# Splitting a group's query products in two and reordering the stretch up to the first output product

## Chip, cores and metric

The kernel runs on one core of one Trainium2 chip. The metric is the device time of one execution in microseconds (us). A core has five engines, each with its own queue of instructions that it works through in order: TensorE (PE in the profile, its weight loads PEld), VectorE (DVE), ScalarE (ACT), GpSimd (POOL) and SyncE (SP), which here issues nearly all transfers. Engines wait for each other through semaphores.

## What is computed

```
a  = S1 x,  b = S2 x            for each row x (32 values) of q and k;  S1, S2: 8 x 32
phi(x) = outer(a, b)            64 features
kv  = sum over s of phi(k_s) v_s     64 x 32,  for each batch (4) and head (4)
z   = sum over s of phi(k_s)
out_s = phi(q_s) kv / (phi(q_s) . z + 1e-6)
X = out as (4352, 128)          4 batches x 1088 rows, 4 heads x 32
H = X @ w_in                    128 x 2048
G = where(H > 0, H, exp(min(H, 0)) - 1)
Y = G @ w_out                   2048 x 128
```

The inputs come as 64-bit floats, so each number of a weight has a low and a high 32-bit word, from which the kernel makes a 32-bit float by bit operations.

## The kernel before

**Tiling.** The 4352 rows are worked in groups of 512 (eight half tiles of 64 rows), the last group shorter. `w_in` and `w_out` are cut into eight chunk pairs `cp` of 2 x 128 columns. For each group and chunk pair `mm1` forms two banks of H (`h`, 128 x 512, one per half `c`), `elu_a` runs two steps on ACT (the negative part, then the exponential), `elu_d` one on DVE (which frees the bank), and `mm2` or `mm2_seven` adds the product with `w_out`. From group 1 on the products with `w_out` go by seven block products in place of eight, whose sums POOL forms.

**Order.** Nothing is scheduled by a program: the kernel is one hand-written list of calls, and each engine gets its instructions in the order of that list. Buffers come from pools: PSUM tag `h` has four banks, `aux` two; an instruction that takes a bank waits until its last reader is done.

**Start.** Keys of batch 0 are turned, multiplied by S1 and S2 and put into kv (`KA_first`, L439, on PE). Then x of group 0 (`xg`) is needed, by two ways that meet:
- the products: `q2_out(0, i)` forms the 64 features of the queries, `q4_early(0, hh)` (L640) turns them on PE, `q4_out(0, hh)` copies them out (on ACT for hh 0, on DVE for hh 1). `KS_copy` (ACT), `KS_turn` (PE, L501) and `KS_out` (ACT, L504) turn kv. `q5_early` (L666) multiplies the two into `xps`.
- the denominators: `q2_prod`, `q2_sum`, `q2_rec` on DVE, `den_wide` (ACT, L648) spreads them, `den_turn` (PE, L656) turns them, `den_out` (ACT, L660) copies them into `dent`.

`q5_early_out(0, w)` (DVE, L678) multiplies `xps` by `dent` for half `w` of the group, and `mm1_first(c, ws)` and `mm1` follow.

**Group 1** has another way: `q1_second` (L549) forms, in eight products, both sketches and the z products of its queries in one bank `abwp`; `q1_second_out` (ACT, L556) copies it; `q2_prod(1)`, `q2_sum(1)`, `q2_rec(1)`, `q2_an(1)` and `q2_out(1, i)` on DVE make the features with the denominators already in them; `q4_early(1, hh)`, `q4_out(1, hh)`, `q5_early(1)` and `q5_early_out(1, w)` make its x. The query rows come to PE's layout by `transp(qT, "q", 0, t0, t1)` on DVE: the first call gives tiles 8 to 12, the second 13 to 16; products i = 0, 1 of `q1_second` read tiles 8 to 11, i = 2, 3 tiles 12 to 15.

**Weights.** `load_rest` has queued their loads on SP. `R1(step, n)` does one rounding step for entry n of `order`: entries 0 and 1 are `w_in` of chunk pairs 0 and 1, 2 and 3 their `w_out`, 4 and 5 `w_in` and `w_out` of pair 2, and 6 to 10 all of pairs 3 to 7. The steps are `strip` (L127 on DVE, L129 on ACT), `low` (ACT L142, or POOL L140), `floor` (DVE L132), `shift` (DVE L135), `round_s` (DVE L119), and `whole` (POOL L145), which gives the finished weight. `whole_half(0, c)` is `whole` for one half of entry 0. SP's next load of a pair (pair 7) waits until the buffer of pair 2 is free, that is for `whole` of entry 5.

Of the kernel before, what the change touches and what calls it, by code (L numbers as in the profile page):

```python
# [12 lines left out]
F32 = mybir.dt.float32  # L13
# [16 lines left out]
def kernel(  # L30
# [21 lines left out]
    nc = tc.nc  # L52
    B, H, S, D = q.shape
    R = S1.shape[0]
    P = 128
# [4 lines left out]
    NT = S // 64  # L60
# [148 lines left out]
    def whole_half(i, c):  # L209
        if wide:  # L210
            cp, w_in, w_out = order[i]
            o = (0 if w_in else 2 * P) + P * c
            whole(raw_w[cp][:, o:o + P], W[:, cp, o:o + P])
# [70 lines left out]
    def transp(dst, x, b, t0, t1):  # L284
        nc.vector.transpose(dst[b][:, t0:t1, :].rearrange("p t (a c) -> p c t a", c=2), hd[x, b][:, :, t0:t1, :])
# [148 lines left out]
    def KA_first(tiles, first, last):  # L434
        if first:
            kv_ps[0] = psum.tile([P, 512], F32, name="kv", tag="o1", bufs=1)
        for i in tiles:
            for h in range(H):
                nc.tensor.matmul(kv_ps[0][32 * h:32 * h + 32, :R * R], vt[0][:, (h * KT + i) * D:(h * KT + i + 1) * D],  # L439
                                 feats[0, i // 5][:, i % 5, h].rearrange("p i j -> p (i j)"),  # L440
                                 start=(first and i == tiles[0]), stop=(last and i == tiles[-1]),
                                 skip_group_check=True, tile_position=(0, 32 * h))
        if last:
            del feats[0, 0], feats[0, 1]
# [51 lines left out]
    def KS_copy():  # L496
        kd = feats["kd"] = work.tile([P, 2, R * R], F32, name="kd", tag="kd", bufs=1)
        nc.scalar.copy(kd[:], _ap(kv_ps[0][:, :R * R], [[0, 2], [1, R * R]]))

    def KS_turn():  # L500
        nc.tensor.transpose(kv_ps[0][:, 128:256], feats.pop("kd")[:].rearrange("p w f -> p (w f)"), ident[:])  # L501

    def KS_out():
        nc.scalar.copy(kvS[:].rearrange("p h d -> p (h d)"), kv_ps[0][:, 128:256])  # L504
# [36 lines left out]
                                 qT[b][:, t, :], SW[:, :, 2, :], skip_group_check=True, tile_position=(0, 64 * u))  # L541
        return p[:, :128].rearrange("p (t h r) -> p h t r", t=4, h=H)

    def q1_second():
        p = psum.tile([P, 512], F32, name="abwp", tag="h", bufs=4)
        for i in range(4):
            for u in range(2):
                b, t = half_tile(1, 2 * i + u)
                nc.tensor.matmul(p[64 * u:64 * u + 64, i * 96:i * 96 + 96], qT[b][:, t, :],  # L549
                                 SW[:].rearrange("p h x r -> p (h x r)"), skip_group_check=True,  # L550
                                 tile_position=(0, 64 * u))
        return p

    def q1_second_out(p):
        abw[1] = work.tile([P, H * 4, 3 * R], F32, name="abw1", tag="abq1", bufs=1)
        nc.scalar.copy(abw[1][:].rearrange("p (h t) y -> p h t y", h=H),  # L556
                       p[:, :384].rearrange("p (t h y) -> p h t y", t=4, h=H))
# [34 lines left out]
    def q2_prod(g, zq=None):  # L592
        m = H * (un[g] if g > 1 else qn[g])
        x = abw[g][:, :m, :]
        pw = pws[g % 2]
        if zq is None:
            nc.vector.tensor_mul(pw[:, :m, :R], x[:, :, R:2 * R], x[:, :, 2 * R:3 * R])
        else:
            nc.vector.tensor_mul(pw[:, :m, :R].rearrange("p (h t) r -> p h t r", h=H),
                                 x[:, :, R:2 * R].rearrange("p (h t) r -> p h t r", h=H), zq)  # L600

    def q2_sum(g):
        m = H * (un[g] if g > 1 else qn[g])
        den = feats["den", g] = work.tile([P, 8 * H], F32, name="den", tag="den")
        nc.vector.tensor_reduce(den[:, :m], pws[g % 2][:, :m], axis=AX, op=ADD)
# [26 lines left out]
    def q4_early(g, hh):  # L632
        if g not in qpT:
            qpT[g] = work.tile([P, H, 2, P], F32, name="qpT", tag="qpT", bufs=2)
        p = qtp[g, hh] = psum.tile([P, 512], F32, name="qtp", tag="aux")
        for h2 in range(2):
            for m in range(2):
                o = (h2 * 2 + m) * P
                r = (2 * hh + h2) * 4 + 2 * m
                nc.tensor.transpose(p[:, o:o + P], qp[g][:, r:r + 2].rearrange("p t i j -> p (t i j)"), ident[:])  # L640

    def q4_out(g, hh):
        (nc.vector.tensor_copy if g == 0 and hh else nc.scalar.copy)(
            qpT[g][:, 2 * hh:2 * hh + 2], qtp.pop((g, hh))[:].rearrange("p (h m s) -> p h m s", h=2, m=2))

    def den_wide():
        d = feats["denw"] = work.tile([P, 4, H, D], F32, name="denw", tag="ob", bufs=2)
        nc.scalar.copy(d[:], _ap(feats.pop(("den", 0))[:, :1], [[1, 4], [4, H], [0, D]]))  # L648

    def den_turn():  # L650
        p = feats["denp"] = psum.tile([P, 512], F32, name="denp", tag="h", bufs=4)
        d = feats.pop("denw")
        for w in range(2):
            for m in range(2):
                o = (2 * w + m) * P
                nc.tensor.transpose(p[:, o:o + P], d[:, 2 * m + w].rearrange("p h d -> p (h d)"), ident[:])  # L656

    def den_out():
        d = feats["dent"] = work.tile([P, 2, 2 * P], F32, name="dent", tag="cc", bufs=1)
        nc.scalar.copy(d[:].rearrange("p w s -> p (w s)"), feats.pop("denp")[:])  # L660

    def q5_early(g):
        xp = xps[g] = [psum.tile([P, 512], F32, name="xps", tag="aux") for _ in range(2)]
        for h in range(H):
            for w in range(2):
                nc.tensor.matmul(xp[w][D * h:D * h + D, :256], kvS[64 * w:64 * w + 64, h, :],  # L666
                                 qpT[g][64 * w:64 * w + 64, h].rearrange("p m s -> p (m s)"),
                                 skip_group_check=True, tile_position=(64 * w, D * h))

    def q5_early_out(g, w):  # L670
        if g not in xg:
            xg[g] = work.tile([P, 512], F32, name="xg", tag="xg", bufs=3)
        to = xg[g][:].rearrange("p (m w s) -> p w m s", w=2, s=P)
        x = xps[g][w][:, :256].rearrange("p (m s) -> p m s", s=P)
        if g:
            nc.scalar.copy(to[:, w], x)
        else:
            nc.vector.tensor_mul(to[:, w], x, feats["dent"][:, w].rearrange("p (m s) -> p m s", s=P))  # L678
# [238 lines left out]
    def mm1_first(c, ws):  # L917
        h = h_tile(0, 0, c)
        for w in ws:
            cols = [x[:].rearrange("p (m w s) -> p w m s", w=2, s=P)[:, w] for x in (h, xg[0])]  # L920
            quarters(cols[0], W[:, 0, c * P:c * P + P], cols[1])
# [138 lines left out]
    transp(qT, "q", 0, 8, 13)  # L1060
    q4_early(0, 0)
    KA_first(range(5, 9), False, True)
    q4_early(0, 1)
    q2_prod(0, zq)
    R1(strip, 0, nc.scalar)
    R1(low, 0)
    R1(strip, 1, nc.scalar)
    q4_out(0, 0)
    transp(qT, "q", 0, 13, NT)
    abwp = q1_second()  # L1070
    q2_sum(0)
    R1(floor, 0)
    KS_copy()
    KS_turn()
    q2_rec(0)
    den_wide()
    den_turn()
    q1_second_out(abwp)
    KS_out()
    R1(floor, 1)  # L1080
    R1(shift, 0)
    R1(shift, 1)
    q4_out(0, 1)
    R1(strip, 2, nc.scalar)
    den_out()
    R1(round_s, 1)
    q5_early(0)
    q2_prod(1)
    R1(low, 1, nc.gpsimd)
    R1(round_s, 0)  # L1090
    whole_half(0, 0)
    q2_sum(1)
    q5_early_out(0, 0)
    R1(low, 2)
    R1(low, 3)
    R1(low, 4)
    R1(strip, 3, nc.scalar)
    q5_early_out(0, 1)
    mm1_first(0, (0,))
    mm1_first(0, (1,))  # L1100
    elu_a(0, 0, 0, (0,))
    R1(strip, 4)
    q2_rec(1)
    R1(floor, 4)
    q2_an(1)
    R1(shift, 4)
    whole_half(0, 1)
    R1(whole, 1)
    mm1_first(1, (0, 1))
    elu_a(0, 0, 0, (1,))  # L1110
    q2_out(1, 1)
    mm1(0, 1, (1,))
    mm1(0, 1, (0,))
    q4_early(1, 1)
    R1(round_s, 4)
    q2_out(1, 0)
    elu_d(0, 0, 0)
    elu_a(0, 0, 1, (0,))
    q4_early(1, 0)
    elu_a(0, 0, 1, (1,))  # L1120
    elu_a(0, 1, 1, (0,))
    elu_a(0, 1, 1, (1,))
    elu_d(0, 0, 1)
    R1(whole, 4)
    mm1(0, 2, (0,))
    mm1(0, 2, (1,))
    R1(floor, 2)
    R1(shift, 2)
    R1(round_s, 2)
    q4_out(1, 1)  # L1130
    q4_out(1, 0)
    R1(strip, 7)
    elu_d(0, 1, 1)
    KT_out(0)
    elu_a(0, 1, 0, (0,))
    R1(floor, 3)
    R1(strip, 5)
    R1(whole, 2)
    elu_a(0, 2, 1, (0,))
    elu_a(0, 1, 0, (1,))  # L1140
    q5_early(1)
    q5_early_out(1, 1)
    q5_early_out(1, 0)
    mm2(0, 0, False, (0,))
    R1(shift, 3)
    R1(floor, 5)
    R1(low, 5)
# [826 lines left out]
```

## Time and profile before

| | us |
|---|---|
| median of 3 runs | 259.83 (259.80 to 260.07) |
| the profiled execution | 260.47 |
| its span | 258.33 |
| PE busy | 251.8 (97% of the span) |
| DVE, ACT, POOL busy | 174.6, 182.0, 184.1 |
| granted clock of PE | 0.997 |

The span is the time from the first to the last instruction of the profiled execution; 2.14 us lie around it. Times of the timeline count from the span's start. In a row of the timeline the first number is the start, the second the time from the first start to the last end of the rows merged (with the count after the x), and what stands in brackets is how long the engine sat idle before it and what it waited for. A 32-bit product on PE appears as two records, a turn by PE as one. Ends of PE's records are modelled.

### The profile page before, as it was taken

The page shows a single profiled execution, that of the slowest core. Times are in us where ns is not written, and L with a number is a line of the kernel's source. Part 1 is how long each engine was busy: PE and PEld are TensorE (multiplying, and loading weights), DVE is VectorE, ACT ScalarE, POOL GpSimd, SP SyncE. Part 2 cuts the span into 40 slices and gives each one's busy share as a digit, 9 for nine tenths or more (in the row PEclk, how much of TensorE's full clock was granted, in tenths as well). Part 3 has the DMA queues.
Part 4 walks back from the last instruction along what each step waited for, and adds up shares of the span by engine and source line. Part 5 has one row for each costly group of instructions (what it writes and reads, how often), then busy time and mean ns, then how long its engine had stood idle before and what let it go on. Part 6 is the DMA issues. An engine that isn't in the chain of part 4 may idle for free.

```text
span 258.3 us, 9778 instructions
## 1 busy us (share of the span) xinstructions
PE 251.8 (97%) x4101; PEld 159.8 (62%) x4101; DVE 174.6 (68%) x342; ACT 182.0 (70%) x357; POOL 184.1 (71%) x236
## 2 busy tenths in 40 slices
PE   8789999999999999999999999999999999999994
PEld 7653333426666677657648466666766666667994
DVE  5898998898859875797658587743455445644651
ACT  2589887748757657676577877578677777777792
POOL 5433365698994978877858887987888888888310
PEclk9999999999999999999999999999999999999998
DMA  6999593313000011114102004312021100110021
GB/s 178 303 366 238 177 285 65 95 23 55 7 5 4 15 18 27 25 35 105 35 13 31 0 7 94 83 39 33 11 32 28 19 3 0 24 20 3 3 33 31
DMA packets 30907, 16.56 MB, mean 64 GB/s; under 512 B 22512, under 2 KB 28016, under 8 KB 30864
## 3 DMA queue, kind: packets, MB, share of 16 engines
q1 hardware_dynamic: 29904, 15.04, 24.4%
q10 hardware_dynamic: 896, 0.84, 1.3%
q8 instruction: 32, 0.52, 0.9%
q14 instruction: 11, 0.09, 0.1%
q0 software_dynamic: 64, 0.07, 0.1%
HBM read 11.21 MB, written 2.36 MB: 53 GB/s over the span
## 4 chain that ended last, share of the span: by engine, by line
PE 94%; DMA 3%; ACTq 1%; ACT 0%; issue 0%; DVE 0%; DVEq 0%
PE h L259 46%; PE pb L839 18%; PE pa L839 15%; PE o L259 5%; PE ol L259 3%; DMA v<-in_v_dram 3%; PE kv L453 1%; PE qtp L640 1%; PE h L738 1%; PE h L574 1%; PE pb L815 1%; PE xps L666 1%; PE kv L439 1%; PE kfps L366 1%; ACTq L81 0%; PE h L726 0%
## 5 line engine op out<-in xcount | busy, mean ns | idle before, releaser
L938 DVE SCALAR_TENSOR_TENSOR gg<-e,h 128x512 f32<-128x512 f32 x128 | 85.8, 682 | 60.9 <-ACT e L932 49.6
L259 PE MATMUL h<-xg,W 128*32 128x512 f32 (+2 forms) x768 | 121.7, 584 | 0.7 <-DVE xg L678 0.7
L930 ACT ACTIVATE e<-h 128x512 f32<-128x512 f32 x128 | 74.7, 591 | 51.3 <-PE h L259 49.7
L795 POOL TENSOR_TENSOR tt<-gg 128x512 f32<-128x512 f32 x55 | 71.5, 1301 | 25.9 <-DVE gg L938 23.2
L932 ACT ACTIVATE e<-e 128x512 f32<-128x512 f32 x128 | 79.3, 630 | 3.2
L259 PEld LDWEIGHTS h<-xg,W 128*32 128x32 f32 (+1 forms) x768 | 34.8, 119 | 44.5 <-issue 32.9
L800 POOL TENSOR_TENSOR tt<-tt,gg 128x256 f32<-128x256 f32 x55 | 41.8, 762 | 3.1
L802 POOL TENSOR_TENSOR tt<-gg,tt 128x256 f32<-128x256 f32 x55 | 40.5, 738 | 3.4
L839 PEld LDWEIGHTS pa<-gg,W 128*64 128x64 f32 (+1 forms) x528 | 25.7, 125 | 25.9 <-issue 25.6
L839 PE MATMUL pa<-gg,W 128*64 128x128 f32 (+1 forms) x528 | 32.4, 273 | 0.0
L839 PE MATMUL pb<-tt,SS 128*64 128x128 f32 (+1 forms) x472 | 29.5, 273 | 0.0
L145 POOL TENSOR_TENSOR W<-W,raw 128x256 uint32<-128x256 uint32 (+2 forms) x12 | 11.6, 977 | 20.3 <-ACT e L932 4.5
L839 PE MATMUL pa<-tt,SS 128*32 128x128 f32 (+1 forms) x404 | 25.3, 273 | 0.0
L839 PEld LDWEIGHTS pb<-tt,SS 128*64 128x64 f32 (+1 forms) x472 | 22.7, 127 | 0.0
L839 PE MATMUL pb<-tt,W 128*64 128x128 f32 (+1 forms) x292 | 21.9, 273 | 0.0
L839 PE MATMUL pb<-gg,SS 128*64 128x128 f32 (+1 forms) x292 | 21.8, 273 | 0.0
L839 PEld LDWEIGHTS pa<-tt,SS 128*32 128x32 f32 (+1 forms) x404 | 17.0, 120 | 0.0
L259 PE MATMUL o<-gg,W 128*32 128x512 f32 x128 | 15.3, 593 | 0.0
L839 PEld LDWEIGHTS pb<-gg,SS 128*64 128x64 f32 (+1 forms) x292 | 13.9, 124 | 0.0
L839 PEld LDWEIGHTS pb<-tt,W 128*64 128x64 f32 (+1 forms) x292 | 13.9, 124 | 0.0
L991 DVE SCALAR_TENSOR_TENSOR gg<-e,h 128x256 f32<-128x256 f32 x16 | 6.6, 418 | 6.4 <-PE h L259 3.2
L259 PEld LDWEIGHTS o<-gg,W 128*32 128x32 f32 x128 | 4.1, 110 | 9.3 <-issue 7.1
(181 smaller groups left out, 268.9 us busy)
## 6 DMA issues: line engine op xcount, KB each, us to landing
raw<-in_moe_w_in_dram SPq DMA_DIRECT2D x8, 256.0 KB, 6.6
raw<-in_moe_w_out_dram SPq DMA_DIRECT2D x8, 256.0 KB, 6.4
raw<-qpF SPq DMA_DIRECT2D x30, 64.0 KB, 2.0
out_dram<-ob SPq DMA_DIRECT2D x112, 16.0 KB, 1.5
hd_k<-in_k_dram SPq DMA_DIRECT2D x3, 544.0 KB, 8.7
hd_q<-in_q_dram SPq DMA_DIRECT2D x3, 544.0 KB, 8.3
v<-in_v_dram SPq DMA_DIRECT2D x4, 288.0 KB, 8.8
v<-in_v_dram SPq DMA_DIRECT2D x3, 256.0 KB, 8.8
```

Source lines behind the costliest of these rows:

```text
L145: nc.gpsimd.tensor_tensor(dst.bitcast(U32), dst.bitcast(U32), words(raw)[0], op=ADD)
L259: nc.tensor.matmul(dst[c:c + tile], lhs[:, c:c + tile], rhs, skip_group_check=True, tile_position=(0, c), **kw)
L366: nc.tensor.matmul(ps[g2][32 * c:32 * c + 32, :32 * KT], Sxp[r].rearrange("p x c r -> p (x c r)"), kT[b][r, u * KT:u * KT + KT, 32 * w:32 ...
L439: nc.tensor.matmul(kv_ps[0][32 * h:32 * h + 32, :R * R], vt[0][:, (h * KT + i) * D:(h * KT + i + 1) * D], feats[0, i // 5][:, i % 5, h].re ...
L795: nc.gpsimd.tensor_tensor(_ap(ts[g, cp][:, 0], [[4 * P, 2], [P, 2], [1, P]]), _ap(gs[g, cp][:, 0, P:], [[4 * P, 2]] + us), _ap(gs[g, cp][: ...
L800: nc.gpsimd.tensor_tensor(t[:, 1], t[:, 2], quarter(g, cp, 0, 0), op=ADD)
L802: nc.gpsimd.tensor_tensor(t[:, 3], quarter(g, cp, 1, 0), t[:, 1], op=SUB)
L839: nc.tensor.matmul(bank[r:r + width[0], P * col:P * col + P], lhs[:, w:w + width[0]], rhs[:, u], start=(first and i in ((0,) if g == 1 els ...
L930: nc.scalar.activation(e, hs[g, cp][c][:, :n], RELU, scale=-1.0)
L932: nc.scalar.activation(e, e, EXP, scale=-1.0)
L938: nc.vector.scalar_tensor_tensor(gs[g, cp][:, c, :n], es[g, cp][:, c, :n], -1.0, hs[g, cp][c][:, :n], op0=ADD, op1=MAX)
L991: nc.vector.scalar_tensor_tensor(gs["last", k // 2][:, k % 2, :2 * P], es["last", k // 2][:, k % 2, :2 * P], -1.0, hs["last", k][:, :2 * P ...
```

## The change

`q1_second` takes a bank and a pair of product numbers, so that it can be called twice: products 0 and 1 directly behind the turns of group 0's features (`q4_early(0, 1)`) and ahead of `KS_turn`, products 2 and 3 behind `q5_early(0)` and ahead of `mm1_first`. No instruction is added or left out on any engine. The list of calls from `q4_early(0, 1)` to the first `mm2` is put in another order; everything behind it stays. For each engine the new order is:

- PE: `q4_early(0,1)`, `q1_second` (0, 1), `KS_turn`, `den_turn`, `q5_early(0)`, `q1_second` (2, 3), `mm1_first` three times, `mm1(0,1)` half 0 then 1, `q4_early(1,0)`, `q4_early(1,1)`, `mm1(0,2)` half 1 then 0, `q5_early(1)`, `mm2(0,0)`.
- ACT: `low` 0, `strip` 0, `strip` 1, `KS_copy`, `den_wide`, `q4_out(0,0)`, `KS_out`, `strip` 2, `den_out`, `strip` 3, `low` 3, `q1_second_out`, `low` 4, `low` 2, then the steps of elu.
- DVE: `floor` 0, `q2_prod(0)`, `shift` 0, `q2_sum(0)`, `q2_rec(0)`, `round_s` 0, `floor` 1, `q4_out(0,1)`, `shift` 1, the transpose of tiles 13 to 16, `round_s` 1, `floor` 2, `q5_early_out(0,0)` and `(0,1)`, `strip` 4, `q2_prod(1)`, `floor` 4, `q2_sum(1)`, `q2_rec(1)`, `q2_an(1)`, `shift` 4, `q2_out(1,0)`, `round_s` 4, `q2_out(1,1)`, `elu_d` of chunk pair 0, and so on.
- POOL: `whole_half(0,0)`, `whole_half(0,1)`, `low` 1, `whole` 1, `whole` 4, `whole` 2 (before: `low` 1 first).

The function, and the list down to the first steps of elu:

```diff
-    def q1_second():
-        p = psum.tile([P, 512], F32, name="abwp", tag="h", bufs=4)
-        for i in range(4):
+    def q1_second(p=None, half=(0, 1)):
+        p = p or psum.tile([P, 512], F32, name="abwp", tag="h", bufs=4)
+        for i in half:
...
+    R1(low, 0)
     q4_early(0, 1)
+    R1(strip, 0, nc.scalar)
+    abwp = q1_second(None, (0, 1))
+    R1(floor, 0)
     q2_prod(0, zq)
-    R1(strip, 0, nc.scalar)
-    R1(low, 0)
+    R1(shift, 0)
     R1(strip, 1, nc.scalar)
-    q4_out(0, 0)
-    transp(qT, "q", 0, 13, NT)
-    abwp = q1_second()
     q2_sum(0)
-    R1(floor, 0)
-    KS_copy()
-    KS_turn()
     q2_rec(0)
-    den_wide()
-    den_turn()
-    q1_second_out(abwp)
-    KS_out()
-    R1(floor, 1)
-    R1(shift, 0)
-    R1(shift, 1)
-    q4_out(0, 1)
-    R1(strip, 2, nc.scalar)
-    den_out()
-    R1(round_s, 1)
-    q5_early(0)
-    q2_prod(1)
-    R1(low, 1, nc.gpsimd)
     R1(round_s, 0)
     whole_half(0, 0)
+    whole_half(0, 1)
+    R1(floor, 1)
+    KS_copy()
+    den_wide()
+    KS_turn()
+    den_turn()
+    q4_out(0, 1)
+    q4_out(0, 0)
+    KS_out()
+    q5_early(0)
+    R1(strip, 2, nc.scalar)
+    R1(shift, 1)
+    transp(qT, "q", 0, 13, NT)
+    abwp = q1_second(abwp, (2, 3))
+    den_out()
+    R1(strip, 3, nc.scalar)
+    R1(round_s, 1)
+    R1(floor, 2)
+    q5_early_out(0, 0)
+    q5_early_out(0, 1)
+    R1(low, 1, nc.gpsimd)
+    R1(whole, 1)
+    mm1_first(0, (0,))
+    R1(low, 3)
+    mm1_first(0, (1,))
+    q1_second_out(abwp)
+    R1(low, 4)
+    R1(low, 2)
+    R1(strip, 4)
+    q2_prod(1)
+    mm1_first(1, (0, 1))
+    mm1(0, 1, (0,))
+    mm1(0, 1, (1,))
...
```

More of the change, by code (lines that the diff above doesn't have):

```diff
@@ L1081 @@
-    R1(shift, 0)
-    R1(shift, 1)
-    q4_out(0, 1)
-    R1(strip, 2, nc.scalar)
-    den_out()
-    R1(round_s, 1)
-    q5_early(0)
-    q2_prod(1)
-    R1(low, 1, nc.gpsimd)
     R1(round_s, 0)
     whole_half(0, 0)
-    q2_sum(1)
[L1093 to L1102, printed above, removed]
+    whole_half(0, 1)
+    R1(floor, 1)
+    KS_copy()
@@ L1103 @@
+    R1(low, 2)
[4 more added lines that the diff above has]
+    mm1(0, 1, (1,))
+    elu_a(0, 0, 0, (0,))
+    elu_a(0, 0, 1, (0,))
+    elu_a(0, 0, 0, (1,))
+    elu_a(0, 0, 1, (1,))
+    R1(floor, 4)
+    q2_sum(1)
     q2_rec(1)
-    R1(floor, 4)
     q2_an(1)
     R1(shift, 4)
[L1107 to L1110, printed above, removed]
+    elu_a(0, 1, 1, (0,))
+    q2_out(1, 0)
+    q4_early(1, 0)
+    elu_a(0, 1, 1, (1,))
@@ L1111 @@
+    R1(round_s, 4)
     q2_out(1, 1)
-    mm1(0, 1, (1,))
-    mm1(0, 1, (0,))
     q4_early(1, 1)
[L1115 to L1129, printed above, removed]
     q4_out(1, 1)
     q4_out(1, 0)
+    R1(whole, 4)
+    elu_a(0, 1, 0, (0,))
+    elu_d(0, 0, 0)
@@ L1132 @@
+    elu_d(0, 0, 1)
+    R1(shift, 2)
+    R1(strip, 5)
+    R1(round_s, 2)
+    mm1(0, 2, (1,))
+    mm1(0, 2, (0,))
+    R1(whole, 2)
+    q5_early(1)
+    mm2(0, 0, False, (0,))
     R1(strip, 7)
     elu_d(0, 1, 1)
+    elu_a(0, 2, 1, (0,))
     KT_out(0)
-    elu_a(0, 1, 0, (0,))
+    q5_early_out(1, 1)
+    elu_a(0, 1, 0, (1,))
     R1(floor, 3)
[L1137 to L1142, printed above, removed]
     q5_early_out(1, 0)
-    mm2(0, 0, False, (0,))
```

## The prediction

> **What bounds the kernel now.** I read the page first, then the chain of waits, then the waits of TensorE, then the timeline from 9 to 31 us.
>
> ```profile
> PE 251.8 (97%) x4101; PEld 159.8 (62%) x4101; DVE 174.6 (68%) x342; ACT 182.0 (70%) x357; POOL 184.1 (71%) x236
> PE 94%; DMA 3%; ACTq 1%; ACT 0%; issue 0%; DVE 0%; DVEq 0%
> ```
>
> TensorE (PE) is busy for 97% of the span and is 94% of the chain. Its own waits are these four:
>
> ```profile
> PE idle L267 <- PEq L1959: 0.8, 1, 0.8
> PE h L259 <- DVE xg L678: 0.7, 1, 0.7
> PE abqp L527 <- DVE qT L285: 0.7, 1, 0.7
> PE kv L439 <- DMA v<-in_v_dram: 0.7, 1, 0.7
> ```
>
> Three lie before 10 us, where the change does nothing. The fourth, the wait for group 0's x (xg), is the last: behind it the stream stays closed to the end. So what the change is worth is how much earlier the first product with x starts, less whatever new hole it opens. The timeline shows what ends that wait:
>
> ```profile
> 12.80 0.88 PE L549 MATMUL abwp<-SW,qT 128*64 128x96 f32 x16
> 13.62 0.33 PE L501 MATMUL kv<-ident,kd 128*128 128x128 f32 x1
> 13.73 0.48 ACT L556 COPY abw<-abwp 128x384 f32<-128x384 f32 x1 [0.54 <-PE abwp L549]
> 13.78 0.60 PE L656 MATMUL denp<-ident,denw 128*128 128x128 f32 x4
> 14.11 0.27 ACT L504 COPY kvS<-kv 128x128 f32<-128x128 f32 x1
> 14.27 0.45 ACT L129 ACTIVATE W<-raw 128x256 f32<-128x256 f32 x1
> 14.43 0.67 PE L666 MATMUL xps<-qpT,kvS 64*32 64x256 f32 x16
> 14.61 0.58 ACT L660 COPY dent<-denp 128x512 f32<-128x512 f32 x1
> 15.26 0.76 DVE L678 TENSOR_TENSOR xg<-xps,dent 128x256 f32<-128x256 f32 x2 [0.17 <-PE xps L666]
> 15.83 3.96 PE L259 MATMUL h<-xg,W 128*32 128x256 f32 x48 [0.73 <-DVE xg L678]
> ```
>
> Sixteen records of group 1's eight query products (L549) stand ahead of the two turns (L501, L656). Their copy (L556) and a strip (L129) stand on ACT ahead of KS_out (L504) and den_out (L660). The first half of x waits for den_out (ends 15.19; x starts 15.26), which is later than the xps product (ends 15.10).
>
> **The change part by part.** Starts follow each other on ACT and DVE by about the duration less 0.1 (the 0.57 copy at 11.95, the next at 12.41); a result reaches ACT or DVE after 0.06, PE after 0.15 (x ends 15.68, PE starts 15.83); a dependent DVE op starts 0.08 behind.
>
> *PE ahead of x.* The first half keeps 8 of 16 records: four pairs at 0.08, so 0.33 less, and the turn of KS starts at 13.29 instead of 13.62, ending 13.62. Its input kd is there: the copy is freed of q4_out(0,0) and starts at KV's end, 12.28 + 0.06 = 12.34, over at 12.61. den_turn's place is 13.45. Its input hangs on q2_prod(0), now behind floor(0) on DVE, and floor(0) waits for strip(0), which goes behind low(0) on ACT (10.08 and 10.51, over at 10.96: in time). So floor 11.36, product 11.55, shift 11.72, sum 11.92, reciprocal 12.27, over at 12.51 (before 12.50, since a transpose left the chain). den_wide is thus where it was, 12.57 to 13.20; 0.15 makes 13.35, in time. den_turn ends 14.05.
>
> *ACT.* q4_out(0,0) 13.10 to 13.67. KS_out 13.67 to 13.94 (before 14.11). The xps products start at 13.99 (PE is free at 13.98), 0.44 earlier, and end at 14.66. strip(2) 13.83, den_out 14.17 to 14.76.
>
> *DVE up to x.* round_s(0) 12.43, floor(1) 12.77, copy q4_out(0,1) 12.95 (its transposes end 12.88), shift(1) 13.55, transpose 13..16, round_s(1), floor(2), then x: 0.28, 0.43, 0.42 and 0.25 less 0.08 each put x's place at 14.62. One wait is added, because POOL now works there: whole_half(0,0) and (0,1) run from 12.99 to 13.87 (0.46 each), then low(1). This row shows what a POOL op does to a DVE op of one tensor and a constant: strip(4), 0.28 elsewhere, took 0.81, ending 0.15 behind POOL's last op (16.59):
>
> ```profile
> 15.93 0.81 DVE L127 TENSOR_SCALAR W<-raw 128x256 uint32<-128x256 uint32 x1
> ```
>
> So shift(1) ends at 13.87 + 0.15 = 14.02 and x's place becomes 14.80. x starts at the latest of 14.80, 14.82 (dent) and 14.72 (xps): 14.82 instead of 15.26. PE's first product starts at 15.39 instead of 15.83: **0.44 gained**. That shift(1) slips in between two POOL ops is the choice here; the bounds are 14.72 (0.54 gained) and 15.22 (it also waits for low(1), 0.04 gained).
>
> The Trainium skill (SBUF — State Buffer, "Who interferes with whom") calls this an exclusive lock of a shared port pair, and holds DVE ops with two SBUF inputs to it as well, against a POOL op that reads SBUF. By that rule round_s(1), due at 14.30, waits for low(1), which itself began behind shift(1) (14.02 to 14.43); x's place becomes 14.90 and the gain 0.36. No row here shows such a DVE op held.
>
> *The second half.* PE has its place behind xps: 13.99 + 0.60 (the L666 at 22.59 to the next at 23.19) = 14.59; the transpose it needs is over at 14.35. Its last pair starts at 14.89, and with the 0.18 of a change of shape (13.43 to 13.62 ahead of L501) PE is free at 15.07. x comes at 15.39, so the half and its switch cost nothing; if x came at once, they would cost 0.48. The Trainium skill (TensorEngine Tiling, "Key Properties") says a change of tiling mode drains TensorE, which speaks against splitting: two more changes. By the rule the second half costs one more drain, by the rows it lies in the wait.
>
> *Behind x, group 1.* q1_second_out moves from 13.73 to 15.40 on ACT (behind strip(3) 14.64 and low(3) 14.98, whose loads landed by 13.0; over 15.88). Behind it wait low(4), low(2), then elu at 16.63, whose h is ready at 16.82: free. On DVE strip(4) is due at 15.5 and held behind whole(1) to 15.8, which costs nothing, since q2_prod(1) waits for that copy: it goes from 14.25 to 15.91, and the chain closes up: floor 16.12, sum 16.30, reciprocal 16.68, an 17.00, shift(4) 17.20, q2_out 17.41, round_s(4) 18.01, q2_out 18.35 to 19.03 (before 19.01). PE wants them at 19.28 and 19.72, so 0.5 is spare.
>
> *The rest to w_out.* First elu_d 18.95 to 19.63, second to 20.23; their banks (the four of tag h are taken here to come round in the order in which they come free) are wanted at 20.30 and 21.16. whole(4) ends 19.60, wanted 20.30; q4_out(1,·) ends 21.61, wanted 22.15; whole(2) about 22.0, wanted 22.75; xg of group 1 24.01, wanted 24.49. KT_out is queued earlier, but its transfers stand on SP behind the weight loads, which hold until 27.41 either way. mm1's halves change order at one price, the same records either way. strip(5) and strip(7) move ahead on DVE, into time that the elu before them leaves (20.35 and 20.90), their loads long landed. After the first w_out the order is the old one and PE closed, so 0.44 reaches the end.
>
> *Sum.* The profiled execution took 260.47: span 258.33 and 2.14 around it. The new span is 257.89, its execution 260.03. The median lies 0.64 under the profiled one, so **259.39**, 0.17% less.
>
> **Rivals.** *B, the columns start level.* From 15.83, 32 records of 256 columns and 16 of 512 should take 3.44 (24 of 512 take 2.57 from 24.93) plus 0.13 for the change to transposes (20.74 to 22.59 less 1.72): 3.57. They took 3.89 (15.83 to 19.72). One record starts at 15.83, the other column groups at 16.14. No producer is shown for this 0.32. For its loss: PE now comes fresh from other products. Against: xg's second half still follows 0.34 behind the first. Then 0.44 + 0.32 = 0.76, **259.07**.
>
> *C, shift(1) waits through low(1).* x starts 15.22, gain 0.04, **259.79**. For: three POOL ops stand back to back. Against: nothing shows that POOL keeps its turn.
>
> *D, slower: DVE's group 1 chain becomes the bound.* Strip(4), floor(4) and shift(4) now stand in the one chain ahead of q2_out, and q4_early(1,·) blocks mm1(0,2) on PE. If each of the three waits behind a POOL op of 0.74 to 1.07 (whole(1), whole(4)), q2_out ends up to 2 us later, 21.0 instead of 19.03. It decides from 0.54 later (19.57), and the kernel is slower from 0.98 later; at 1.5 later, a loss of 0.52, **260.35**. For: strip(4) was held before, and its cover (the spread of this chain from 14.25 on) is gone. Against: POOL has only whole(1) and whole(4) between 14.9 and 19.6.
>
> That the change does nothing is C's time.
>
> **How the numbers follow.** A 0.45, B 0.25, C 0.10, D 0.20. Under 0.2% (0.52 us) no measurement of this kernel tells a change from none. A spans 0.3 to 0.6, one third of it over 0.52: 0.15 faster, 0.30 same. B is faster (0.25). C is 0.08 same and 0.02 slower. D is slower (0.20). So 0.40, 0.38 and 0.22. The range runs from 259.0 (B, with 0.07 for the spread of runs) to 260.2, which takes in C and the lower part of D and leaves out about 0.15. A's own range is 259.2 to 259.55.
>
> **What would show it.** Right: KS_out at 13.7, xps at 14.0, den_out at 14.2, x at 14.8, the first h at 15.4, no hole in PE behind it, and L549 in two stretches at 12.8 and 14.6. Wrong: x behind 15.0 with a long L135 on DVE beside POOL's L140 (C); transposes L640 of group 1 or mm1(0,2) behind a wait for DVE near 19.7 (D); columns level at the first h (B). A hole in PE after 23 us would make all of it wrong.

## The result, and the profile after

| | before | after |
|---|---|---|
| median of 22 runs each | 259.82 us | 259.18 us |
| ratio of the times, 95% interval | | 0.9971 [0.9961, 0.9980] |
| the profiled execution | 260.47 us | 259.66 us |
| its span | 258.33 us | 257.76 us |

The kernel is faster by 0.29%: by 0.75 us, between 0.52 and 1.01, if the ratio is laid on 259.82. (One run of after, 262.79 us at a granted clock of 0.987 where the others show 0.997 to 1.0, was disturbed and is not in the ratio.)

First the page of after, its line of busy time and the one of the chain. They hardly moved, and PE still carries the chain:

```profile
PE 252.1 (98%) x4101; PEld 159.6 (62%) x4101; DVE 174.6 (68%) x342; ACT 182.1 (71%) x357; POOL 183.8 (71%) x236
...
PE 93%; DMA 4%; DVE 1%; issue 0%; ACTq 0%; SPq 0%; ACT 0%
```

Next PE's waits in after. The third row is the one that counts: the wait for x, 0.7 before, is 0.3, and no new wait for DVE or ACT stands beside it. The others lie ahead of 10 us.

```profile
PE abqp L527 <- DVE qT L285: 0.9, 1, 0.9
PE idle L267 <- PEq L1960: 0.8, 1, 0.8
PE h L259 <- DVE xg L678: 0.3, 1, 0.3
PE kv L439 <- issue: 0.2, 1, 0.2
```

Last the timeline of after, the rows that answer to those of before, with the turns of group 0's features (L640 at 12.18, 12.22 before) as the mark to count from, and POOL's two rows:

```profile
12.18 0.66 PE L640 MATMUL qtp<-ident,qp 128*128 128x128 f32 x4
...
12.77 0.55 PE L549 MATMUL abwp<-SW,qT 128*64 128x96 f32 x8
...
12.91 0.88 POOL L145 TENSOR_TENSOR W<-W,raw 128x128 uint32<-128x128 uint32 x2 [2.09 <-DVE W L119]
...
13.25 0.33 PE L501 MATMUL kv<-ident,kd 128*128 128x128 f32 x1
13.42 0.60 PE L656 MATMUL denp<-ident,denw 128*128 128x128 f32 x4
13.49 0.45 DVE L135 TENSOR_SCALAR W<-W 128x256 uint32<-128x256 uint32 x1
13.62 0.27 ACT L504 COPY kvS<-kv 128x128 f32<-128x128 f32 x1
13.76 0.48 POOL L140 TENSOR_SCALAR raw<-raw 128x256 f32<-128x256 uint32 x1
...
13.95 0.66 PE L666 MATMUL xps<-qpT,kvS 64*32 64x256 f32 x16
14.13 0.57 ACT L660 COPY dent<-denp 128x512 f32<-128x512 f32 x1
...
14.54 0.55 PE L549 MATMUL abwp<-SW,qT 128*64 128x96 f32 x8
...
14.77 0.76 DVE L678 TENSOR_TENSOR xg<-xps,dent 128x256 f32<-128x256 f32 x2
...
15.34 3.87 PE L259 MATMUL h<-xg,W 128*32 128x256 f32 x48 [0.25 <-DVE xg L678]
...
19.15 1.09 PE L640 MATMUL qtp<-ident,qp 128*128 128x128 f32 x8
```

The eight query products stand in two stretches of 0.55. KS_out (L504) follows at 13.62 in place of 14.11, den_out (L660) at 14.13 in place of 14.61, x (L678) at 14.77 in place of 15.26, the first h at 15.34 in place of 15.83. Counted from the mark, the profiles give:

| us | before | after | |
|---|---|---|---|
| mark to first h | 3.61 | 3.16 | -0.45 |
| first h to group 1's transposes | 3.89 | 3.80 | -0.09 |
| mark to first w_out product (L259, o<-gg) | 10.97 | 10.44 | -0.53 |
| from there to PE's end | 231.52 | 231.53 | +0.01 |

With the 0.04 by which the mark itself came earlier, upstream of the change, this is the span's 0.57. What the change does is over at the first w_out product.

### The profile page after: what moved, and what is told of

It reads as the page before. It is cut to its first block, busy times and chain, and to the rows that moved or that the text cites. A ratio compares the mean times of both kernels' runs of the same rounds, so it can differ in the third digit from the quotient of the medians.

```text
span 257.8 us, 9779 instructions
## 1 busy us (share of the span) xinstructions
PE 252.1 (98%) x4101; PEld 159.6 (62%) x4101; DVE 174.6 (68%) x342; ACT 182.1 (71%) x357; POOL 183.8 (71%) x236
## 4 chain that ended last, share of the span: by engine, by line
PE 93%; DMA 4%; DVE 1%; issue 0%; ACTq 0%; SPq 0%; ACT 0%
PE h L259 46%; PE pb L839 18%; PE pa L839 15%; PE o L259 5%; PE ol L259 3%; DMA hd_q<-in_q_dram 2%; PE kv L453 1%; DMA hd_k<-in_k_dram 1%; PE h L738 1%; PE h L574 1%; PE pb L815 1%; PE kfps L366 1%; PE h L726 0%; PE qtp L640 0%; DVE qT L285 0%
## 5 line engine op out<-in xcount | busy, mean ns | idle before, releaser
L259 PE MATMUL h<-xg,W 128*32 128x512 f32 (+2 forms) x768 | 121.6, 584 | 0.3 <-DVE xg L678 0.3
L259 PEld LDWEIGHTS h<-xg,W 128*32 128x32 f32 (+1 forms) x768 | 34.5, 119 | 43.9 <-issue 32.3
L259 PE MATMUL o<-gg,W 128*32 128x512 f32 x128 | 15.3, 593 | 0.0
L259 PEld LDWEIGHTS o<-gg,W 128*32 128x32 f32 x128 | 4.1, 110 | 9.3 <-issue 7.1
```

The source lines that it names most:

```text
L259: nc.tensor.matmul(dst[c:c + tile], lhs[:, c:c + tile], rhs, skip_group_check=True, tile_position=(0, c), **kw)
```

## The experiments

Twelve runs followed, of nine further kernels: e8 and e11 are e2 again, e12 is the changed kernel again. The 22 runs of before lie between 259.07 and 260.55 us. The distance from the mark to h repeated within 0.07 us where one kernel was profiled more than once (3.16 twice; 3.09, 3.15 and 3.09), and the one to w_out within 0.17, so each run is read first by its distances; most have one profile. "Pause" is the delay between the first product with x and those of the other column groups. "KV start" is where KV's products begin, all of them upstream of the change. Each ratio is against runs of before taken alongside (medians of 259.82 to 259.91).

| | mark to h | pause | h to transposes | mark to w_out | KV start | median us (runs) | ratio to before |
|---|---|---|---|---|---|---|---|
| before | 3.61 | 0.32 | 3.89 | 10.97 | 9.76 | 259.82 (22) | |
| after | 3.16 | 0.23 | 3.80 | 10.44 | 9.73 | 259.18 (22) | 0.9971 [0.9961, 0.9980] |
| e1_split_alone | 3.16 | 0.59 | 4.16 | 10.79 | 10.08 | 259.61 (12) | 0.9992 [0.9976, 1.0008] |
| e2_all_behind | 3.09 | 0.01 | 3.58 | 10.14 | 8.87 | 259.59 (12) | 0.9986 [0.9971, 1.0002] |
| e3_old_tail | 3.16 | 0.32 | 3.89 | 10.52 | 10.00 | 259.33 (12) | 0.9980 [0.9962, 0.9997] |
| e4_first_by_half | 3.15 | 0.16 | 3.72 | 10.34 | 9.56 | 259.15 (12) | 0.9975 [0.9960, 0.9989] |
| e5_low_early | 3.27 | 0.29 | 3.86 | 10.60 | 9.14 | 259.27 (1) | |
| e6_all_front | 3.49 | 0.15 | 3.72 | 10.68 | 9.96 | 259.24 (12) | 0.9984 [0.9970, 0.9998] |
| e7_more_start | 3.17 | 0.01 | 3.58 | 10.22 | 11.03 | 260.73 (12) | 1.0019 [0.9997, 1.0042] |
| e8_all_behind_again | 3.15 | 0.11 | 3.68 | 10.30 | 9.61 | 259.47 (1) | |
| e9_after_16 | 3.31 | 0.01 | 3.58 | 10.36 | 9.24 | 259.26 (12) | 0.9972 [0.9959, 0.9986] |
| e10_before_16 | 3.62 | 0.01 | 3.58 | 10.67 | 9.03 | 259.93 (12) | 1.0000 [0.9984, 1.0016] |
| e11_all_behind_3 | 3.09 | 0.01 | 3.58 | 10.14 | 9.24 | 259.24 (8) | 0.9975 [0.9962, 0.9989] |
| e12_changed_again | 3.16 | 0.17 | 3.73 | 10.36 | 9.75 | 260.45 (1) | |

### The split or the order: e1 and e6

e1 is the kernel before with the split alone; group 1's chain, which can't run until the second half is copied, goes behind it:

```diff
-    abwp = q1_second()
+    abwp = q1_second(None, (0, 1))
...
-    q1_second_out(abwp)
...
-    q2_prod(1)
+    abwp = q1_second(abwp, (2, 3))
...
-    q2_sum(1)
...
+    q1_second_out(abwp)
...
+    q2_prod(1)
+    q2_sum(1)
```

> The old order with the split alone: products 0 and 1 of q1_second in the old place, 2 and 3 behind q5_early(0); what depends on them is moved with them and nothing else is (q1_second_out behind low(2) on ACT, q2_prod(1) and q2_sum(1) behind x and strip(4) on DVE). Theory S (the split and the freed ACT and DVE places make the gain, the rest of the new order adds nothing): KS_turn 0.33 earlier at 13.29, KS_out at 13.7, xps at 14.0, den_out at 14.2, x at 14.8, first h at 15.35 to 15.4 as in the changed kernel (15.34), and the whole 0.45 to 0.6 us under the kernel before. Theory O (the reordering of the rounding steps makes it): first h not before 15.6, less than 0.3 us gained.

e6 is the changed kernel with all eight products in front again, and ahead of them the transpose that the last four read; the order is else the new one:

```diff
-    abwp = q1_second(None, (0, 1))
+    transp(qT, "q", 0, 13, NT)
+    abwp = q1_second(None, (0, 1, 2, 3))
...
-    transp(qT, "q", 0, 13, NT)
-    abwp = q1_second(abwp, (2, 3))
```

> The new order without the split: all eight query products of group 1 ahead of KS_turn, with the transpose of tiles 13 to 16 moved ahead of floor(0) on DVE because they need it. Theory S: PE's turn of KS is 0.33 later again and the denominators' chain 0.36 later (the transpose), den_wide 12.9, den_out about 14.5, x about 15.15, first h 15.7: 0.1 to 0.2 us under the kernel before. Rival O (the order is what gains): first h by 15.45 and 0.45 us or more gained.

PE's timeline of e1, and below it that of e6:

```profile
12.53 0.66 PE L640 MATMUL qtp<-ident,qp 128*128 128x128 f32 x4
...
15.69 4.23 PE L259 MATMUL h<-xg,W 128*32 128x256 f32 x48 [0.25 <-POOL W L145]
19.85 1.09 PE L640 MATMUL qtp<-ident,qp 128*128 128x128 f32 x8
```

```profile
12.41 0.66 PE L640 MATMUL qtp<-ident,qp 128*128 128x128 f32 x4
...
15.90 3.79 PE L259 MATMUL h<-xg,W 128*32 128x256 f32 x48 [0.73 <-DVE xg L678]
19.63 1.09 PE L640 MATMUL qtp<-ident,qp 128*128 128x128 f32 x8
```

15.69 less 12.53 is 3.16, the changed kernel's distance to the hundredth: the split brings the whole 0.45 without the new order. (The row names POOL as the releaser; x began at 15.12, 0.57 ahead of the product, as in after.) The order without the split gives 15.90 less 12.41, 3.49, which is 0.12 less than before, and leaves the wait for x at 0.73. In e6 the 16 records still stand ahead of the turn of KS, which starts 1.40 behind the mark as before, but the two ACT ops are gone from in front of KS_out: it starts 1.77 behind the mark against 1.89. That is the 0.12; the other 0.33 is the records. Both together bring 0.45 and no more. But e1 loses 0.27 of it again in the stretch from h to the transposes (4.16 against 3.89), all of it the pause, and its time can't be told from before. (Its one profile, of 260.89, is the slowest of its twelve runs.) Whether the old order lengthens the pause in most executions isn't shown.

### Must it be two halves: e2, e8, e11

All eight products behind xps, none in front; the three are the same kernel, run at three times:

```diff
-    abwp = q1_second(None, (0, 1))
...
-    abwp = q1_second(abwp, (2, 3))
+    abwp = q1_second(None, (0, 1, 2, 3))
```

> The changed kernel with all eight query products of group 1 in the second place, behind q5_early(0) and ahead of mm1_first, none ahead of KS_turn. By the prediction's rows: KS_turn can start at 12.95 (its kd is there at 12.6), den_turn is held by den_wide (13.15 + 0.15 = 13.3), KS_out by q4_out(0,0) on ACT (13.5), so xps at 13.85 to 13.95, hardly earlier than 13.95. Behind it PE is busy with the products to 14.45 + 0.7 + 0.18 = 15.35, x is there at 15.2 to 15.3: first h 15.3 to 15.4, the same time as the changed kernel within 0.1 us. If the split itself matters (PE becomes the bound in front of h): first h later than 15.5 and 0.2 us or more lost against the changed kernel.

> The kernel with all eight query products behind q5_early(0) once more, for a second profile: in the first the start of KV came 0.9 us earlier than in the profile before. If the level start of the columns (no pause at record 449, 3.58 to the transposes) belongs to this kernel, it shows again, and 10.1 to 10.2 us lie between q4_early(0,1) and the first w_out product. If it belongs to the early start of that execution (the 16 KB piece of instructions had 3 us to come), the pause is back, 0.15 to 0.4 us, and 10.3 to 10.5 lie between them.

> The kernel with all eight query products behind q5_early(0) a third time, timed in five rounds more: from q4_early(0,1) to the first w_out it took 10.14 and 10.30 us in two profiles against 10.44 for the changed kernel, but its 12 timed runs gained only 0.14% (0.29 to -0.02). If the profiles are right, 10.1 to 10.3 again and 0.25% to 0.35% under the kernel before. If the time is right, the stage is longer in most executions: 10.5 or more in this profile, and 0.1% to 0.2%.

PE's timeline of e11:

```profile
11.69 0.66 PE L640 MATMUL qtp<-ident,qp 128*128 128x128 f32 x4
12.19 0.29 PE L501 MATMUL kv<-ident,kd 128*128 128x128 f32 x1
12.70 0.66 PE L656 MATMUL denp<-ident,denw 128*128 128x128 f32 x4 [0.22 <-ACT denw L648]
13.35 0.67 PE L666 MATMUL xps<-qpT,kvS 64*32 64x256 f32 x16
13.95 0.88 PE L549 MATMUL abwp<-SW,qT 128*64 128x96 f32 x16
14.78 3.65 PE L259 MATMUL h<-xg,W 128*32 128x256 f32 x48
```

The first h comes 3.09 behind the mark (3.15 in e8), no later than with two halves. PE now waits 0.22 for den_wide, where the first half stood, and not at all for x: x begins at 14.22, its product 0.56 later, and the 16 records fill the time before it exactly. So what x's way needed on PE was to be rid of products ahead of the two turns; the half that the change leaves in front costs 0.07 at most. The distance to w_out is 10.14 to 10.30, below the 10.36 and 10.44 of the changed kernel, mostly by the pause. e8 fits neither of its two forecasts: its pause of 0.11 lies between none and 0.15. The times don't show a difference: the intervals of 0.9986 and 0.9975 both take in 0.9971. Whether this form is the faster one stays open.

### The end of the new order: e3

The changed kernel, with the order of before from the second call of `mm1_first(1, ·)` to the first w_out (elu, `q2_out`, `mm1(0,1)` and `mm1(0,2)`, `R1` as before):

```diff
-    mm1(0, 1, (0,))
-    mm1(0, 1, (1,))
...
-    elu_a(0, 1, 1, (0,))
-    q2_out(1, 0)
-    q4_early(1, 0)
...
     q2_out(1, 1)
+    mm1(0, 1, (1,))
+    mm1(0, 1, (0,))
     q4_early(1, 1)
...
+    q2_out(1, 0)
...
+    q4_early(1, 0)
...
```

> The changed kernel down to mm1_first, then the old order from the first elu to the first w_out. Theory S: x and the first h as in the changed kernel (15.34), and the old tail keeps PE closed as well, so transposes of group 1 and w_out come at the same distance behind the first h and the time is that of the changed kernel within 0.1 us. Rival (the new tail is needed, because group 1's chain on DVE now starts 1.6 us later): a hole of 0.3 us or more in PE at q4_early(1,1) or at mm1(0,2), and the gain shrinks to under 0.3 us.

First h at 3.16, and from there to the transposes 3.89, the same as before; PE has no hole. The 0.08 between its 10.52 and 10.44 is the pause again (0.32 against 0.23). By these distances the order behind the first h is worth nothing either way.

### What holds shift(1): e5

`low(1)` on POOL goes ahead of the two `whole_half`, so that nothing stands behind them on POOL:

```diff
+    R1(low, 1, nc.gpsimd)
     R1(round_s, 0)
     whole_half(0, 0)
...
-    R1(low, 1, nc.gpsimd)
```

> The changed kernel with low(1) first on POOL (as before the change), ahead of whole_half(0,0). It takes away the POOL op that can follow whole_half(0,1) while shift(1) waits on DVE. Theory L (a DVE op of one tensor and a constant waits for the POOL op that is running): low(1) runs by 12.1, shift(1) still starts beside whole_half(0,1) and ends about 0.15 behind it, 0.40 to 0.45 long as now; x starts within 0.05 of the changed kernel counted from the second turns of group 0 (2.59 from q4_early(0,1) to x), since den_out ends only 0.08 ahead of x. Rival (in the changed kernel low(1) holds shift(1)): shift(1) becomes 0.28 long and x comes 0.1 to 0.15 earlier.

POOL and DVE in e5's timeline:

```profile
10.99 0.45 POOL L140 TENSOR_SCALAR raw<-raw 128x256 f32<-128x256 uint32 x1 [0.83 <-DVE W L132]
11.05 0.54 DVE L135 TENSOR_SCALAR W<-W 128x256 uint32<-128x256 uint32 x1
...
12.50 0.88 POOL L145 TENSOR_TENSOR W<-W,raw 128x128 uint32<-128x128 uint32 x2 [1.06 <-ACT kd L498]
13.08 0.45 DVE L135 TENSOR_SCALAR W<-W 128x256 uint32<-128x256 uint32 x1
```

shift(1) (L135 at 13.08) takes 0.45, as it does with `low(1)` behind it, and ends 13.53, 0.15 behind POOL's 13.38. In after it ended 13.94, 0.15 behind 13.79. So in these two executions `whole_half` holds it and the `low(1)` behind doesn't. But which POOL op holds it can change from one execution to the next. In e12, the changed kernel once more, both `whole_half` were over at 13.42, and `low(1)` was running when shift(1) began:

```profile
13.39 0.43 POOL L140 TENSOR_SCALAR raw<-raw 128x256 f32<-128x256 uint32 x1
...
13.51 0.46 DVE L135 TENSOR_SCALAR W<-W 128x256 uint32<-128x256 uint32 x1
```

It ended 13.97, 0.15 behind `low(1)`'s 13.82; e3, e6 and e7 show `low(1)` holding it too (0.51 to 0.56). In all eleven profiles with the new order shift(1) ended 0.14 to 0.15 behind the last POOL op that had begun ahead of it, and didn't wait for one that began later.

In e5 the price only moved: shift(0) (L135 at 11.05) now took 0.54, beside `low(1)`, where it took 0.28 in after. Counted from the mark (11.60 in e5), shift(1) began 0.17 later than in after and the first h came 0.11 later.

### The pause between the column groups: e4, e7, e9, e10, e12

e4 asks for the first halves of x by both chunks before any second half:

```diff
     mm1_first(0, (0,))
...
-    mm1_first(0, (1,))
+    mm1_first(1, (0,))
...
-    mm1_first(1, (0, 1))
+    mm1_first(0, (1,))
+    mm1_first(1, (1,))
```

> The changed kernel with the first products by halves of x: mm1_first(0, first half), mm1_first(1, first half), then the second half for both, so that the wait for the second half of x stands 16 records behind the start instead of 8. Theory W (the 0.23 to 0.32 us by which three column groups start late at the first h comes from the weight load that waits for the second half of x): the columns start level, 15.34 to the transposes of group 1 takes 3.57 to 3.6 instead of 3.81, and the end comes 0.2 us earlier than in the changed kernel. Theory P (it is PE's own, at a start behind a wait): 3.8 as before and no gain.

0.16 of pause were left, with nothing there that reads the second half, and 0.17 are left in e12 without this edit. The wait for x's second half isn't its cause.

e7 adds four 8-column products (eight records of products, eight of weight loads) to the products that run at the start; e9 and e10 add the same number ahead of KV, e9 to the changed kernel and e10 to the kernel before:

```diff
+    keep_warm(4, 8)                                            # e7, behind keep_warm(1, 224)
+    quarters(feats["z"][:, 256:264], SXh[:], zl[:, :8])        # e9, e10, behind Z(0, ...)
```

> The changed kernel with four more products of 8 columns behind the warming products at the start (16 more records on PE, where it waits for S1 and S2 until 4.2). It tests the pause at the first h: in five profiles the matmul behind record 448 of PE waits 0.14 to 0.59 us, always the same record, also where the wait in front of it is another. Theory F (the pause belongs to the place in PE's instruction stream, at which a 16 KB piece of instructions begins): it moves 16 records forward, into the second half of the query products, where PE has 0.25 us to spare; the columns start level at the first h, 3.57 to 3.62 from there to the transposes of group 1 instead of 3.80, and the kernel is 0.2 us faster than the changed one. Theory W (it belongs to the first h and what that waits for): the pause stays at the second column group of the first h, 3.7 to 3.9.

> The changed kernel with four products of 8 columns more (16 records on PE) behind Z of batch 0, ahead of KV, where PE waits for v; they write columns of that bank that nobody reads. It moves everything behind them by 16 places in PE's instruction stream without making it later. Theory F (the pause at the first h belongs to a place in the stream, records 433 to 449 of the changed kernel): the pause now falls 16 records earlier, into the second half of the query products, where 0.25 us are spare; the column groups start level at the first h (under 0.05 us apart), 3.57 to 3.62 us from there to the transposes of group 1 (3.80 in the changed kernel), 10.2 from q4_early(0,1) to w_out (10.44), and the time is 0.2 us under the changed kernel's. Theory W (the pause belongs to the first h and to a start behind a wait): 0.1 to 0.4 us between the column groups as before, 3.7 to 3.9, no gain.

> The kernel before with the same 16 records ahead of KV. Theory F: its pause of 0.32 us at the first h goes too (it falls into the xps products or into the wait for x, which is 0.73 us long): 3.57 to 3.62 from the first h to the transposes of group 1 instead of 3.89, and 0.3 us gained on the kernel before without the change. Theory W: 3.8 to 3.9 and no gain.

PE's timelines of e10 and of e9:

```profile
15.08 3.65 PE L259 MATMUL h<-xg,W 128*32 128x256 f32 x48 [0.73 <-DVE xg L678]
18.66 1.09 PE L640 MATMUL qtp<-ident,qp 128*128 128x128 f32 x8
```

```profile
14.05 0.38 PE L549 MATMUL abwp<-SW,qT 128*64 128x96 f32 x3
14.62 0.46 PE L549 MATMUL abwp<-SW,qT 128*64 128x96 f32 x5 [0.19 <-issue]
15.01 3.65 PE L259 MATMUL h<-xg,W 128*32 128x256 f32 x48
18.59 1.09 PE L640 MATMUL qtp<-ident,qp 128*128 128x128 f32 x8
```

In e10 the program differs from before only in four products that nobody reads, 6 us earlier; x and its wait (0.73) are as they were, and the pause is gone: 3.58 in place of 3.89. In e9 it is gone from the first h too, but a hole has opened inside the second half of the query products, behind its third record: from the start of xps to x's product PE needs 1.55 in place of 1.39. In e7 the added records took some 0.19 each so early (5.15 in place of 3.65 for the row at 0.78), and KV started 1.3 later than in after; seven of its twelve runs, the profiled one among them, took 260.69 to 261.63 us, the other five 259.25 to 259.61, so this delay isn't in every execution. Its columns were level as well. So the pause isn't a wait for x. The number of instructions ahead may move it, but each of these is one profile, and that number isn't all: e2 and e11 have no pause with the unchanged number ahead, and e8, the same kernel, has 0.11.

Before and e9 would fit a fixed place in PE's stream: the pause falls behind the 212th record of a product in the one, behind the 214th in the other (those that warm PE left out, the added ones counted). But in e10 that place lies in the xps products, whose row (0.67) is as long as before, and in e7 in the second half of the query products, whose row (0.55) is as long as in after. That a piece of the instructions comes late at that place was the guess. In all fourteen profiles the last piece of 16 KB in the queue "instruction" ahead of the first h had ended by then (in after at 14.31, with the first h at 15.34 and the pause over at 15.57). Yet how long before goes with the pause: 2.65 to 3.36 us in e2, e7, e10 and e11, which have none, and 0.86 to 2.55 in the nine that have one; e9, with 1.77, has its hole. That speaks for something that arrives, but it is no proof, and the length of the pause doesn't follow it (0.29 in e5 at 2.55, 0.11 in e8 at 1.61). The cause stays open. Its loss also bought nothing that can be measured: e10 saves 0.30 to w_out, and its ratio of 1.0000 [0.9984, 1.0016] allows a gain of up to 0.42 us. A gain of 0.30 may be in it; it isn't shown.

e12 is the changed kernel once more, for the spread of its distances.

> The changed kernel once more, for a second profile of the same instructions: from q4_early(0,1) to x 2.59 and to the first h 3.16 again within 0.05 us, since semaphores and fixed durations set them; the pause at the first h anywhere from 0 to 0.4 us if it is set by something that arrives (instructions), 0.23 again if it is set by the program's own waits.

Mark to h was 3.16 again and the pause 0.17, but the one execution took 260.45. This row of its view of line L738, far behind the change, says where that went: a wait at 125 us for a transfer, which after doesn't have.

```profile
  DMA raw<-qpF: 0.5, 1
```

From the first w_out to PE's end e12 needed 232.32 us against 231.53 in after, 0.8 more; e1 needed 0.33 more and e9 0.14, at the same place.

## Why the prediction was right

**The main step held to 0.05 us.** Each station of the way to x came out where the sum put it, less the 0.04 by which the whole execution was early: KS_turn 13.25 (13.29 forecast), den_turn 13.42 (13.45), KS_out 13.62 (13.67), xps 13.95 (13.99), den_out 14.13 (14.17), x 14.77 (14.82), first h 15.34 (15.39). The gain was 0.45 against 0.44.

**The wait that was added had its forecast size.** shift(1) was to end 0.15 behind `whole_half`, between two POOL ops, and did (13.94 against 14.02 less 0.04); `low(1)` then took 0.48. Rival C, in which it waits through `whole_half` and `low(1)` one behind the other, fell there and in e5. That `whole_half` was the op that held it is the chance of this execution: in e12 it was `low(1)` alone, at the same price.

round_s(1), of two inputs, began at 14.22, with `low(1)` ending at 14.24, so it met next to nothing of it and the gain was not cut to 0.36. The prediction says that no row here shows such an op held. Later rows of the profile of before do: q2_prod of a later group (L597) reads both its inputs from SBUF, where the kernel's tiles outside PSUM lie, and so do these POOL ops.

```profile
55.76 0.74 POOL L800 TENSOR_TENSOR tt<-tt,gg 128x256 f32<-128x256 f32 x1
55.81 0.97 DVE L597 TENSOR_TENSOR pw<-abw 128x256 f32<-128x256 f32 x1
...
133.55 0.42 DVE L597 TENSOR_TENSOR pw<-abw 128x256 f32<-128x256 f32 x1
133.71 1.40 POOL L795 TENSOR_TENSOR tt<-gg 128x512 f32<-128x512 f32 x1 [2.76 <-DVE gg L938]
```

Where it began ahead of POOL's op it took 0.42; where it began 0.05 behind one it took 0.97 and ended 0.28 behind it. The Trainium skill (SBUF — State Buffer, "Who interferes with whom") holds DVE ops with two SBUF inputs to the lock as well. These rows agree with it.

**The second half was free where it was put.** It lay at 14.54 (14.59 forecast), and PE still waited 0.25 behind it. The split adds one change of shape, not the two of the prediction: from the mark to h PE's rows change shape four times before and five times after. The Trainium skill (TensorEngine Tiling (Array Packing), "Key Properties") has each change of tiling mode drain TensorE. The one further change lay inside that wait, so no run here shows its price. e9 shows where that ends: with the hole in it the half was over 0.48 later, the 0.25 were used up, and h came 0.15 later from the mark.

**Group 1's chain stayed ahead of PE.** Strip(4) 15.44, q2_prod(1) 15.86, q2_out from 17.30 to 18.91, elu_d 18.84, against a forecast of 15.8, 15.91, 17.41 to 19.03 and 18.95; the transposes took it at 19.15 without a wait. Rival D needed POOL to hold strip(4), floor(4) and shift(4); each took 0.28, so none was held.

**The mis-sized terms.** The forecast was 259.39 and the median is 259.18, 0.21 less and just under A's own range (259.2 to 259.55). One term was taken as unchanged and wasn't: the pause between column groups, 0.32 before and 0.23 and 0.17 in two profiles of the changed kernel. That is 0.09 and 0.15 of the 0.32 that rival B set on it, and B itself fell, since the columns didn't start level. The span came out 0.13 under its forecast (257.76 against 257.89): 0.09 is the pause, 0.04 the earlier mark. The rest is the scatter of single executions, and that it stayed small is luck: the time around the span was 1.90 in place of 2.14, and the median of after lies 0.48 under its profiled execution in place of 0.64. In the profiles the span fell by 0.57, the medians by 0.64, and the ratio says 0.52 to 1.01. That the two spans differ by nearly the change alone is luck as well: KV started at 9.76 and 9.73 in them, and e12, the changed kernel again, took 0.8 more around 125 us. Of the chances, that for "within 0.2%" rested on A alone being worth 0.17%; with the pause's 0.09 the sum is 0.53, just over the bound of 0.52.

Two things that the prediction leaned on turned out not to be needed. Up to the first h the new order, costed step by step, brings nothing that the split in the old order didn't (e1), and the front half needn't be there (e2, e11). Behind the first h it isn't settled: e1's interval (0.9976 to 1.0008) hardly meets that of the changed kernel (0.9961 to 0.9980). What the prediction called the gain, records and two ACT ops that stood ahead of the turns and their copies, is what these variants take away; in e6, which takes away the ACT ops alone, 0.12 of the 0.45 comes and the wait for x stays at 0.73.

## What to carry to other kernels

Where two ways meet, look in each engine's queue for work of a later stage that stands ahead of them, and put it where the engine would wait for the meeting point anyway; that wait is the room it may fill, and what exceeds it delays the result. When the gain is near the scatter of the runs, compare distances between two rows of one trace, and try the pieces of a reorder by themselves before crediting the whole.

## What the runs showed of the hardware

- PE paused for 0.11 to 0.59 us among the first products with x in nine of the fourteen profiles. The three with four unread products far ahead have no pause there, but neither have two of the three of e2's kernel without them. The cause is open.
- A DVE op of one tensor and a constant (shift(1), 0.28 alone) that began beside a POOL op took 0.38 to 0.56 and ended 0.14 to 0.15 behind the last POOL op that had begun ahead of it, in eleven profiles. In six of them, after among them, another POOL op came right behind; the DVE op got in between, and that POOL op took 0.48 to 0.50 where it takes 0.42 to 0.45.
- A DVE op of two SBUF inputs (L597, 128x256) took 0.97 in place of 0.42 when it began 0.04 to 0.05 behind a POOL op of two SBUF inputs, in before and in after.
- Two places that the change doesn't touch differ from one execution to the next by as much as it brings or more: KV's start (8.87 to 10.08 in the profiles, e7 left out) and the stretch around 125 us (0 to 0.8 us more).
